# Expert slots in two tiles of 128, routed in three steps inside the attention, and partial value products in place of copies

## The chip, the cores and the metric

One core of a Trainium2 chip. The metric is the device time of one execution in microseconds (us), taken as the median of the runs shown; shorter is better.

## The reference

Attention over 4 batches, 8 heads, 768 positions, head width 64. Three heads (0, 2, 6) attend to every earlier position; the other five, the streaming heads, only to the last 64 positions and to positions 0 to 3. Then every token (3072 rows of 512 values) may pass through one of 8 experts:

```python
scores = where(mask, (q @ k.T) / sqrt(64), -1e9)
x = (softmax(scores) @ v)              # 3072 x 512 after the heads are joined
do_compute = x @ w_skip > 0            # the other tokens leave as they are
logits = x[do_compute] @ w_gate        # 8 experts, the largest is taken
y = gate * (relu(x @ w1[e]) @ w2[e])   # w1: 512 x 1024, w2: 1024 x 512
out[do_compute] = x[do_compute] + y
```

All inputs are float32; the kernel works in float16 with float32 sums.

## The kernel before

**The order of work is planned.** Each piece of work is registered with `op(name, engine, duration, function, deps, key)` or `dma(...)`. `Plan.lay` then runs a small list scheduler over these durations: on each engine, of what is ready, the piece with the smallest `key` goes first. The program is written in the order of the planned start times, and each engine works through its own list in that order. A wait on the chip therefore holds everything behind it on that engine. `fill` keeps weight loads from running far ahead of other transfers, and `pl.quiet` names two stretches in which no weight load is started: from the last pair's logits to the last attention write, and from the slot numbers (`idx`) to the second gather.

**Attention** runs over 16 pairs of heads, four pairs a batch (`i`, lines 701 to 1005). For each pair:

- `q`, `k` (queue of SyncE, buffers for four pairs) and `v` are loaded and cast to float16 on POOL (`cast` L690, `cast_v` L696), turned by TensorE (L715, L726), and copied out of PSUM: `q` by ACT (L741), `k` in two halves by DVE (L749), each half into a tile whose other 64 rows are zero.
- The gate's logits are carried along: `v` times the gate's weights (L778) stands beside the values in `va` (L785), ten columns for each head, so that the product with the attention weights yields rows, sums and logits at once.
- For streaming heads, `copy_kx` (L760, L761) builds keys for the previous block's second half with the four sink positions in front, and `copy_vx` (L796, L798) builds the same for the values: rows 64 to 127 from the previous block, rows 0 to 63 from block 0. Both on POOL.
- Scores (masks L853, products L865) go to PSUM in pieces of 1024 columns, ACT takes the exponential (L875), `weigh` (L920) multiplies with the values; every product there has all 128 rows.
- DVE takes the reciprocal of the sums (L939), scales logits (L946) and rows (L956). After a batch's last pair `g_sum` (L983) adds up its logits and SyncE's queue writes its rows to `out` (L977). The last batch is written in four parts, after pairs 13, 14 and 15 (twice).

**Routing** comes in two steps: batches 0 to 2 (18 chunks of 128 tokens) as filler in the last pairs, batch 3 (6 chunks) after the attention. A step finds each token's expert (`mx` to `oh`), its rank among the tokens of that expert by products with a triangle and with ones (`ranks`, L1055 to L1062), and then two tables, `L` (the rank as one of 128 positions) and `R` (the expert's tile, with token number and gate). The product of the two (`slots`, L1152) is the list of tokens by slot; `fin` (L1204 to L1207) makes `idx` and `gsl` of it. Each expert has 256 slots, two tiles of 128; tile `t` belongs to expert `t // 2`.

**Experts.** `swap` closes the pools of the attention and lays the expert's buffers over them: ten tiles of weights stay outside, the others and all gathered rows lie in the old attention memory. `gather` (L1239) fetches 128 rows of `out` by `idx`, one indirect transfer a tile on POOL, into rows zeroed by ACT (L1234). For each expert: cast (L1266), four transposes (L1275), copy (L1286); the first layer with both tiles at once, 256 columns, `hps` (L1295); ReLU on ACT (L1306); the second layer tile by tile, `yps` (L1317), always after the next expert's first layer; scaling and adding on DVE (L1323); `scatter` back to `out` (L1252).

**Weights** 0 to 13 (two for each expert, 2 MB of float32 each) are loaded and cast by POOL's queue (L479); 0 to 8 have room during attention, 9 lies in the old `v` buffer, the rest wait for `swap`. Weights 14 and 15 come as float32 on SyncE's queue (L1354), are staged in the space of experts 0 and 1 once these are done, and are cast by ACT and DVE (L1364, L1362).

Of the kernel before, what the change touches and what calls it, by code (L numbers as in the profile page):

```python
# [19 lines left out]
H = 8  # L20
# [25 lines left out]
CH = 1024  # L46

# [5 lines left out]
class Plan:  # L53
# [26 lines left out]
    def lay(self, rings):  # L80
# [30 lines left out]
        while n < len(self.ops):  # L111
            best = None
            for eng, c in ready.items():
                ts = [x for x in map(at, c) if x is not None]
                if ts:
# [7 lines left out]
                    key=lambda o: (o["key"], o["seq"]))  # L123
# [265 lines left out]
def kernel(  # L389
# [54 lines left out]
    cnt = const.tile([P, 2, E + 1], FP16, name="cnt")  # L444
# [15 lines left out]

    for e in range(2):
        t = wpool.tile([P, 2, DS * F], FP16, tag=f"w_{e}", name=f"w_{e}")
        for half in range(2):
            wts[e, half] = t[:, half]
    for n in range(4, NPRE):
        wtile(n, wpool)
# [21 lines left out]
    with tc.tile_pool(name="sm", bufs=1) as sm_pool, \  # L488
         tc.tile_pool(name="tr_ps", bufs=2, space=bass.MemoryType.PSUM) as tr_psum, \
         ExitStack() as pools, ExitStack() as pools2:  # L490

        def pool(name, stack=pools, **kw):
            return stack.enter_context(tc.tile_pool(name=name, **kw))

        ldq_pool = pool("ldq", bufs=1)
# [3 lines left out]
        st_psum = pool("st_ps", bufs=2, space=bass.MemoryType.PSUM)  # L499
# [3 lines left out]
              for n in range(2)]  # L503
# [4 lines left out]
        vxb = [qk_pool.tile([P, 2, NQB - 2, VA], FP16, name=f"vx{n}")  # L508
               for n in range(2)]
# [91 lines left out]
        def c_route():  # L601
# [10 lines left out]
            nc.gpsimd.memset(c24[:, :, 1:2], float(NC) / P)  # L612

        op("route0", "POOL", 2.2, c_route, [("Cv", 3)], 31)

        def c_route1():
            nc.vector.tensor_copy(iota16, tmpi)
            nc.vector.tensor_scalar(C.erev, tmpi[:, :E], -1.0, float(E),
                                    ALU.mult, ALU.add)
            nc.vector.tensor_copy(val[:, :, 1], tmpc)  # L620
            nc.vector.tensor_copy(val[:, :, 0], tmpp.to_broadcast([P, NC]))
# [17 lines left out]
        def load_qk(i, w, eng):  # L639
            def go():  # L640
                b, hs = heads(i)
                t = ldq_pool.tile([P, 2, NQB, D], FP32, tag=w + "f", bufs=NLD,
                                  name=w + "f")
# [13 lines left out]
        NLD = 4  # L657
        sp = iter(range(1000))
        for i in range(NPR):
            for w in "qk":  # L660
                act = i == 0 and w == "k"
                dma(("ld", w, i), "ACT" if act else "SP", 0.45, 1.07,
# [38 lines left out]
        for i in range(NPR):  # L701
            for w in "qk":
# [4 lines left out]
               [("ldv", 0, 1) if 0 < i < 4 else ("ldv", i // 4), ("PV", i - 3, 1), ("Vx", i - 3), "vones"],  # L707
# [37 lines left out]
        def out_k(i, hi):  # L745
            def go():
                r = slice(hi * D, (hi + 1) * D)
                to, ti = in_order(kz[i % 2][hi][r], tps["k", i][r])
                nc.vector.tensor_copy(to, ti)  # L749
# [40 lines left out]
        def copy_vx(i):  # L790
            def go():
                va, vx = vab[i % 3], vxb[i % 2]
                for hi in range(2):
                    if not retr(i, hi):
                        c = slice(hi * VA, (hi + 1) * VA)
                        nc.gpsimd.tensor_copy(  # L796
                            vx[D:, hi], va[D:, 1:NQB - 1, c])
                        nc.gpsimd.tensor_copy(  # L798
                            vx[:D, hi], va[:D, 0:1, c].to_broadcast(
                                [D, NQB - 2, VA]))  # L800
            return go

# [6 lines left out]
        for i in range(NPR):  # L809
# [7 lines left out]
            for hi in range(2):  # L817
                op(("Ok", i, hi), "DVE", 0.96, out_k(i, hi),
# [4 lines left out]
            op(("Tv", i), "PE", 0.36, transpose_v(i), [("Cv", i), "ident"],  # L823
# [6 lines left out]
            op(("Vx", i), "POOL", 0.95 * nx, copy_vx(i),  # L830
               [("Ow", i), ("PV", i - 2, 1)], k0 + 5)
# [67 lines left out]
        def weigh(i, hi):  # L899
            def go():  # L900
# [4 lines left out]
                va, vx = vab[i % 3], vxb[i % 2]  # L905
                vc = slice(hi * VA, (hi + 1) * VA)
                todo = []
                for qb in range(NQB):
                    if retr(i, hi):
                        todo += [(qb, RCOL[j, qb], va[:, j, vc])  # L910
                                 for j in range(qb + 1)]
                    else:
                        todo.append((qb, qb * P, va[:, qb, vc]))
                        if qb == 1:
                            todo.append((qb, NQB * P, va[:, 0, vc]))
                        elif qb:
                            todo.append((qb, (NQB - 1 + qb) * P,
                                         vx[:, hi, qb - 2]))
# [560 lines left out]
```

## Time and profile before

| | |
|---|---|
| median of 3 runs | 201.43 us (200.89 to 211.31) |
| the profiled execution | 200.39 us |
| its span, first to last instruction | 198.9 us |
| granted TensorE clock, mean over the span | 0.902 |
| TensorE busy | 151.8 us (76%) |
| POOL busy | 125.8 us (63%) |
| DVE busy | 115.3 us (58%) |
| ACT busy | 105.3 us (53%) |
| read from and written to DRAM | 56.64 MB, 10.49 MB |

"Busy" is the time in which an engine has at least one instruction in work; PE is TensorE, PEld its loading of weights. A name such as L1295 is a line of the kernel. In a group, the last column is the idle time of the engine just before, and what ended it. In a listing in order of time, each line has its start, its length, engine, line, operation, what is written and read, and in brackets the idle time before. Shares are over the whole span and hide that its stages have different limits, so they are read stage by stage.

### The profile page before, as it was taken

What the parts mean: (1) busy time and instruction counts of PE and PEld (TensorE: products, weight loads), DVE (VectorE), ACT (ScalarE), POOL (GpSimd) and SP (SyncE); (2) the same over time, 40 slices, a digit from 0 to 9 for tenths busy, and PEclk for the clock granted to TensorE, in tenths of its full rate; (3) what the DMA queues carried; (4) which work ended last, traced back from release to release, by engine and by line L of the source; (5) the groups of instructions that cost most, each with busy time, mean ns of one, the idle gap of its engine ahead of it and who ended that gap; (6) DMA issues with size and microseconds to landing.
All of it is one profiled execution on the core that took longest, in us unless ns stands there. A gap on an engine that the chain in (4) does not pass through costs nothing.

```text
span 198.9 us, 4630 instructions
## 1 busy us (share of the span) xinstructions
PE 151.8 (76%) x1832; PEld 119.5 (60%) x1832; DVE 115.3 (58%) x244; ACT 105.3 (53%) x137; POOL 125.8 (63%) x212
## 2 busy tenths in 40 slices
PE   0696789998999999999220027999999759699940
PEld 0475678787888888788220015978669247374810
DVE  6728687699788887998893033392664601304330
ACT  2178359986799789898389001534134013076500
POOL 7445997999889999986954187877835230101740
PEclk9999999999999999999955555899999957999995
DMA  4999999899989999999999439999999999960210
GB/s 158 320 340 347 339 376 331 279 308 338 340 224 356 268 331 212 213 278 282 237 276 250 82 85 243 272 192 285 269 340 405 244 247 269 242 162 9 72 64 15
DMA packets 28240, 49.21 MB, mean 247 GB/s; under 512 B 5156, under 2 KB 21412, under 8 KB 26930
## 3 DMA queue, kind: packets, MB, share of 16 engines
q0 software_dynamic: 5728, 19.45, 43.8%
q1 hardware_dynamic: 21152, 28.97, 43.3%
q10 hardware_dynamic: 1330, 0.41, 0.9%
q8 instruction: 16, 0.26, 0.6%
q14 instruction: 14, 0.11, 0.2%
HBM read 56.64 MB, written 10.49 MB: 337 GB/s over the span
## 4 chain that ended last, share of the span: by engine, by line
PE 45%; issue 20%; POOL 10%; DMA 8%; DVE 7%; SPq 3%; ACT 3%; POOLq 1%; ACTq 0%; DVEq 0%
PE hps L1295 10%; PE pst L865 9%; PE opsa L920 6%; PE yps L1317 6%; PE pst L853 6%; DMA kf<-in_k_dram 4%; PE tps L715 4%; POOL out_dram L1252 3%; DMA out_dram<-x 2%; DVE k L749 2%; SPq L644 2%; POOL q L690 2%; PE tps L726 2%; DMA xg<-out_dram,idx 2%; PE xtp L1275 2%
## 5 line engine op out<-in xcount | busy, mean ns | idle before, releaser
L875 ACT ACTIVATE at<-pst 128x1024 f16<-128x1024 f32 (+1 forms) x60 | 58.4, 1013 | 14.0 <-PE pst L865 13.1
L1306 ACT ACTIVATE ht<-hps 128x512 f16<-128x512 f32 x32 | 19.1, 597 | 55.4 <-PE hps L1295 46.4
L1295 PE MATMUL hps<-xT,w 128*128 128x256 f16 x256 | 34.8, 301 | 5.4 <-DMA w<-in_moe_w_dram 5.4
L865 PE MATMUL pst<-qT,k 128*128 128x128 f16 (+2 forms) x308 | 36.7, 240 | 2.1 <-ACT qT L741 0.9
L1295 PEld LDWEIGHTS <-w 128*128 128x128 f16 x256 | 31.0, 149 | 9.4 <-DMA w<-in_moe_w_dram 6.4
L1252 POOL DMA_INDIRECT out_dram<-xg,idx x16 | 16.5, 1034 | 29.2 <-issue 13.8
L749 DVE COPY k<-tps 64x768 f16<-64x768 f16 x32 | 30.4, 952 | 7.0 <-PE tps L715 6.6
L865 PEld LDWEIGHTS <-k 128*128 128x128 f16 x308 | 24.9, 101 | 11.0 <-DVE k L749 2.5
L1317 PE MATMUL yps<-w,ht 128*128 128x512 f16 x128 | 29.1, 379 | 0.2 <-ACTq L1441 0.2
L1239 POOL DMA_INDIRECT xg<-out_dram,idx x16 | 17.3, 1079 | 12.0 <-issue 11.7
L1323 DVE SCALAR_TENSOR_TENSOR xg<-yps,gsl,xg 128x512 f32<-128x512 f32 x16 | 12.0, 750 | 21.1 <-PE yps L1317 20.8
L853 PE MATMUL pst<-smask,identb 128*128 128x512 bf16 (+2 forms) x64 | 22.1, 356 | 0.2 <-ACT at L875 0.2
L920 PE MATMUL opsa<-va,at 128*128 128x74 f16 x392 | 19.5, 196 | 1.5 <-DVE x L956 1.5
L1317 PEld LDWEIGHTS <-ht 128*128 128x128 f16 x128 | 12.3, 98 | 13.6 <-issue 0.5
L920 PEld LDWEIGHTS <-at 128*128 128x128 f16 x472 | 18.0, 97 | 2.0 <-DVE x L956 1.8
L1286 DVE COPY xT<-xtp 128x512 f16<-128x512 f16 x16 | 6.3, 422 | 19.9 <-PE xtp L1275 19.5
L1266 DVE CAST x<-xg 128x512 f16<-128x512 f32 x16 | 9.9, 640 | 13.1 <-issue 10.0
L479 POOL DMA_DIRECT2D w<-in_moe_w_dram x22 | 12.8, 581 | 6.7 <-DMA w<-in_moe_w_dram 6.0
L741 ACT COPY qT<-tps 128x768 f16<-128x768 f16 x16 | 12.8, 800 | 7.2 <-PE tps L715 7.2
L1275 PE MATMUL xtp<-ident,x 128*128 128x128 f16 x64 | 6.0, 236 | 12.9 <-DVE x L1266 12.9
L696 POOL CAST va<-vf 128x768 f16<-128x768 f32 x16 | 13.3, 829 | 1.6 <-PE opsa L920 0.7
L956 DVE TENSOR_TENSOR x<-opsa,recs 128x768 f32<-128x768 f32 x15 | 14.2, 946 | 0.0
(128 smaller groups left out, 241.9 us busy)
## 6 DMA issues: line engine op xcount, KB each, us to landing
w<-in_moe_w_dram POOLq DMA_DIRECT2D x16, 512.0 KB
qf<-in_q_dram SPq DMA_DIRECT2D x16, 384.0 KB, 5.7
w<-in_moe_w_dram POOLq DMA_DIRECT2D x6, 1024.0 KB
kf<-in_k_dram SPq DMA_DIRECT2D x15, 384.0 KB, 6.1
out_dram<-x SPq DMA_DIRECT2D x7, 768.0 KB, 9.9
w<-in_moe_w_dram SPq DMA_DIRECT2D x4, 1024.0 KB, 13.3
kf<-in_k_dram ACTq DMA_DIRECT2D x1, 384.0 KB, 4.6
vf<-in_v_dram SPq DMA_DIRECT2D x1, 384.0 KB, 5.5
```

The lines of the kernel that those rows point to most:

```text
L696: nc.gpsimd.tensor_copy(vab[i % 3][:, :, GX:GX + 2 * D].rearrange("p n (h d) -> p h n d", h=2), fp32_of("v", i))
L749: nc.vector.tensor_copy(to, ti)
L853: nc.tensor.matmul(pst[:, c0 - c * CH:c0 - c * CH + m].rearrange("p (n c) -> p n c", c=P), identb, mv, start=(n == 0), stop=(n == last))
L865: nc.tensor.matmul(pst[:, c0 - c * CH:c0 - c * CH + m * P], lt, qTs[i][:, qb * P:(qb + m) * P], start=(n == 0), stop=(n == last))
L875: nc.scalar.activation(ats[i][:, c * CH:c * CH + cn], psts[i, c][:, :cn], ACT.Exp, scale=SCALE)
L920: nc.tensor.matmul(opss[i][:, hi, qb * VA:(qb + 1) * VA], ats[i][:, b0 + c:b0 + c + P], vb, start=(n == 0), stop=(n == len(todo) - 1))
L956: nc.vector.tensor_mul(xsb[i // 4][:, :, h0 * D:(h0 + 2) * D].rearrange("p n (h d) -> p h n d", h=2), summed(i, GX, 512 - GX, D), recs[:, ...
L1239: h = nc.gpsimd.indirect_dma_start(out=M.xgs[:, t], out_offset=None, in_=out[:, :], in_offset=bass.IndirectOffsetOnAxis(ap=idx[:, t:t + 1] ...
L1252: h = nc.gpsimd.indirect_dma_start(out=out[:, :], out_offset=bass.IndirectOffsetOnAxis(ap=idx[:, t:t + 1], axis=0), in_=M.xgs[:, t], in_of ...
L1295: nc.tensor.matmul(hps[:, fi, :], w1[:, s, 2 * f2 + fi], xTs[e][:, s, :], start=(fi == 0 and s == 0), stop=(fi == 1 and s == DS - 1))
L1306: nc.scalar.activation(hts[e][:, 2 * f2:2 * f2 + 2], hpss[e, f2], ACT.Relu)
L1317: nc.tensor.matmul(ypss[t], hts[e][:, j, s2 * P:(s2 + 1) * P], w2[:, j], start=(j == 0), stop=(j == FS - 1))
```

## The change

- **Values.** `copy_vx` and its buffers go. In a streaming head each product with such a copy becomes two into the same sum: rows 64 to 127 of the previous block, and rows 0 to 3 of block 0.
- **Slots.** An expert's two tiles are now `t = e` and `t = 8 + e`. The first 128 tokens of an expert fill tile `e`, counted over batches 0 to 2 alone; what is left of these and batch 3 go to tile `8 + e`.
- **Routing** has three steps: batches 0 and 1 (12 chunks, after pair 7), batch 2 (6 chunks, after pair 11), batch 3 (6 chunks). After step 1 the list of tiles 0 to 7 is complete. Step 2 needs only tiles 8 to 15; it starts each expert's count at `base1`, and has fewer operations. Each step has PSUM results of its own, added up in SBUF.
- **Experts** run in the order of `GR`: tile 0 to 3 of experts 0 to 3, each alone with 128 columns in the first layer; then tiles 8 to 11 of the same experts; then experts 4 to 7 with both tiles. Tiles 0 to 7 are gathered once batch 2 is written and step 1 is done; they go into the memory in which `q` and `k` arrived. The first layer uses the PSUM of the scores and may start after the last exponential; the second layer waits for `swap`. The hidden values of the first four lie in a buffer of the attention weights.
- **Copies of `k`.** For pairs 12 to 15 the second half's copy moves from DVE to ACT.
- **Writes.** The last batch goes out in three parts instead of four: 384 columns after pair 14, and twice 128 after pair 15.
- **Weights.** `quiet` is empty. Weights 14 and 15 are staged in four pieces where weights 8 to 11 lay, so each waits for expert 4 or 5 to be done with both tiles. `fill` lets weights from 7 on run 4 us ahead instead of 3, and this from weight 7 instead of 9.

The diff, cut:

```diff
+STEPS = ((0, 12), (12, 6), (18, 6))
+NSPLIT = 4
...
+        OK_ACT = (12, 13, 14, 15)
...
-                nc.vector.tensor_copy(to, ti)
+                (nc.scalar.copy if act else nc.vector.tensor_copy)(to, ti)
...
-        def copy_vx(i):
...
-                        nc.gpsimd.tensor_copy(
-                            vx[D:, hi], va[D:, 1:NQB - 1, c])
-                        nc.gpsimd.tensor_copy(
-                            vx[:D, hi], va[:D, 0:1, c].to_broadcast(
-                                [D, NQB - 2, VA]))
...
-                            todo.append((qb, (NQB - 1 + qb) * P,
-                                         vx[:, hi, qb - 2]))
+                        c = (NQB - 1 + qb) * P
+                        todo += [(qb, c, slice(D, P), qb - 1), (qb, c, slice(N_SINK), 0)]
+                for n, (qb, c, r, j) in enumerate(todo):
                     nc.tensor.matmul(
                         opss[i][:, hi, qb * VA:(qb + 1) * VA],
-                        ats[i][:, b0 + c:b0 + c + P], vb,
+                        ats[i][r, b0 + c:b0 + c + P], va[r, j, vc],
...
-        for i, u, c0, c1, took in ((13, None, 0, 256, 2.2), (14, None, 256, 384, 1.3),
+        for i, u, c0, c1, took in ((14, None, 0, 384, 3.1),
                                    (15, 0, 384, 512, 0.65), (15, 1, 384, 512, 0.65)):
...
+                "base": lambda: v.tensor_scalar(
+                    base1[:, :E], T[1, "rk"][:, n * E:(n + 1) * E], -float(P), 0.0,
+                    ALU.add, ALU.max),
...
-        for ph, c0, n, k0, last in ((0, 0, 18, 140, ("Gs", 2)),
-                                    (1, 18, 6, 150, ("Gs", 3))):
+        for (ph, (c0, n)), (k0, k1), last in zip(
+                enumerate(STEPS), ((105, 110), (130, 125), (150, 165)),
+                (("Gs", 1), ("Gs", 2), ("Gs", 3))):
...
+            for nm in (["rsel", "rank", "h128", "r16", "tt", "oht", "b8", "a8", "ob", "oa"],
+                       ["rsel", "base", "rank", "h128", "r16", "tt", "oht"],
+                       ["rsel", "place"])[ph]:
...
+        GR = [(e, (e,)) for e in range(NSPLIT)] + [(e, (E + e,)) for e in range(NSPLIT)]
+        GR += [(e, (e, E + e)) for e in range(NSPLIT, E)]
+        TO = [t for _, ts in GR for t in ts]
...
+                    hpss[g, u // 2] = st_psum.tile([P, CH], FP32, tag="pst", name="hps")
...
+                        T["hA"] = at_pool.tile([P, RLEN + SLEN], FP16, tag="at", name="hA")
...
+            dma(("G", t), "POOL", 1.1, 0.45, gather(t),
+                ["z" if ROW[t] >= NROW else None,
+                 *([("idx", 2), *X3] if t >= E else [("idx", 1), ("xo", 2, 0), ("xo", 2, 1)]),
...
+                (125 + x if t < NSPLIT else 400 + x), first=True)
...
+        STAGE = {(14, 0): 8, (14, 1): 9, (15, 0): 10, (15, 1): 11}
...
+                    [(prev, "go"), *(("Y", t, 1) for t in (e, E + e)),
...
+            k0 = 600 + 10 * g if t >= NSPLIT else 130 + x
+            op(("cx", t), "DVE", 0.62, cast_x(t), [("G", t), ("tx", back), "tables"], k0)
+            op(("tx", t), "PE", 0.25, turn_x(t), [("cx", t), ("ox", back)],
+               k0 - 15, take=("tps", ("ox", t)))
...
+                op(("F", g, u), "PE", 1.28 if len(ts) == 1 else 0.88, first(g, u),
+                   [("ox", ts[-1]), ("W", 2 * e, 0), ("W", 2 * e, 1),
                     *(("W", 2 * e, c // 2, c) for c in range(4)),
+                    ("X", NPR - 1, nch(NPR - 1) - 1)], k0,
+                   take=("pst", ("Re", g, u + 1)) if u % 2 == 0 else None)
...
-        pl.quiet = [(("Nl", NPR - 1), (("xo", 3, 15, 1), "go")),
-                    ("idx", (("G", 1), "go"))]
+        pl.quiet = []
```

## The prediction

> **What bounds the kernel now.** I read the 40 slices first, then busy time by stage, then the groups by shape, then the stretch between attention and the experts in order of time. The slices:
>
> ```profile
> PE   0696789998999999999220027999999759699940
> PEclk9999999999999999999955555899999957999995
> DMA  4999999899989999999999439999999999960210
> ```
>
> A slice is 4.97 us. TensorE is full to slice 19, nearly empty for four slices, then full again with one dent. The transfer engines are full nearly always; their one hole is slices 22 and 23. The granted clock is halved through the empty slices and one beyond.
>
> ```profile
> 60.00:80.00 20.00, 19.86 (x345) 17.02 (x342) 16.69 (x31) 17.53 (x21) 18.77 (x39) 1.00 1.06 288
> 80.00:97.40 17.40, 15.60 (x279) 13.38 (x280) 16.09 (x41) 12.67 (x15) 13.96 (x29) 1.00 1.06 255
> 97.40:121.00 23.60, 3.24 (x43) 2.56 (x43) 10.52 (x30) 10.34 (x21) 12.76 (x13) 0.53 0.77 179
> 121.00:157.00 36.00, 36.00 (x272) 27.71 (x271) 19.13 (x43) 11.89 (x20) 22.44 (x25) 0.93 1.02 288
> 157.00:177.40 20.40, 15.03 (x94) 10.90 (x93) 3.01 (x5) 4.44 (x8) 3.55 (x4) 0.83 1.00 242
> 177.40:191.40 14.00, 13.72 (x79) 7.91 (x77) 4.97 (x8) 8.37 (x11) 5.28 (x5) 1.00 0.13 44
> ```
>
> The columns are stretch, length, busy time of PE, weight load, DVE, ACT and POOL, clock, DMA share, GB/s. Attention (to 97.4) is bound by PE, 19.86 of 20 us. From 97.4 to 121.0 PE works 3.24 of 23.60 us. The experts are bound by PE to 157, by the arrival of weights to 177.4, and by PE again to 191.4. So there are two limits of almost one length, PE and the transfers, and both have their hole in the same place. What ends last in it:
>
> ```profile
> 97.43 0.23 DVE L939 RECIPROCAL recs<-opsa 128x12 f32<-128x12 f32 x1 [0.18 <-PE opsa L920]
> 98.96 1.35 DVE L1074 TENSOR_TENSOR r_sub<-glog,r_mx 128x48 f32<-128x48 f32 x1
> 107.03 0.19 DVE L1205 SCALAR_TENSOR_TENSOR idx<-msb 128x16 int32<-128x16 f32 x1
> 113.84 1.10 POOL L1239 DMA_INDIRECT xg<-out_dram,idx  x1 [7.09 <-issue]
> 117.33 1.15 DVE L1266 CAST x<-xg 128x512 f16<-128x512 f32 x2 [10.01 <-issue]
> 121.17 5.11 PE L1295 MATMUL hps<-xT,w 128*128 128x256 f16 x24
> ```
>
> Slots are known at 107.2, but the first gather waits until 113.84 for the last attention rows to land in DRAM (the chain of waits has that transfer from 101.86), and the first expert product comes 7.3 us after the gather.
>
> **Partial products.** The second value copies (20 x 0.43 + 20 x 0.43 us, 17.2 us of POOL) go. I credit nothing: POOL, 18.77 of 20 us busy, stands behind a PE that is fuller. If POOL were the true bound, up to 2 us more would be won in the last two batches. In exchange each of 80 products on 128 rows becomes two, on rows 64 to 127 and 0 to 3. A run of 32 such products takes 1.07 us in the chain of waits, 33 ns each, so 80 x 33 ns = +2.7 us of PE, hidden by nothing.
>
> ```profile
> L920 PE MATMUL opsa<-vx,at 128*128 128x74 f16 x80 | 7.9, 195 | 0.0
> L796 POOL COPY vx<-va 64x296 f16<-64x296 f16 x20 | 8.6, 432 | 1.9 <-DVE va L785 1.0
> L1295 PEld LDWEIGHTS <-w 128*128 128x128 f16 x256 | 31.0, 149 | 9.4 <-DMA w<-in_moe_w_dram 6.4
> L865 PEld LDWEIGHTS <-k 128*128 128x128 f16 x308 | 24.9, 101 | 11.0 <-DVE k L749 2.5 <-issue 2.3
> ```
>
> Every shape in the trace reads 128*128; it shows no product on fewer rows. From below: the two halves run side by side, +0 (a gain is excluded, since no product is saved). From above: each change of row count (full, 64, 4, full: 3 x 80 = 240) lets a product run out its 195 ns where 33 would do, 240 x 162 ns = +38.9 us. I take 2.7, by the nearest rows, and keep both ends.
>
> [...]
>
> **Routing in three steps.** Before the last PV, PE now issues ranks and slots of step 0 (12 + 13 products) and of step 1 (9 + 6), 40 against 18 rank products of the old first step. Eighteen slot products took 1.15 us (102.72), 64 ns each: 40 x 64 - 1.15 = +1.4 us. DVE: the old first step's rows add up to 5.5 us; steps 0 and 1 (12 and 6 chunks, the same rows scaled, plus a 0.95 us placement and the slot arithmetic) come to about 9, +3.5; against it four of the `k` copies (0.95 us) leave DVE, -3.8. They land on ACT as 4 x 0.80 = 3.2 us in the last four pairs, where ACT was busy 12.67 of 17.40; if those copies come on the path they cost up to those 3.2. So attention ends at 97.4 + 2.7 + 1.4 = 101.5.
>
> **The first four expert halves.** They need batch 2's rows in DRAM and step 1's slots. Batch 2's last normalization ended at 82.2; shifted by 3 and with the write's usual 9.9 us to landing that gives 95. Step 1 starts at about 84; the old first step took 11.6 us to its ranks among attention's DVE work, the new one is keyed ahead of the last pairs, so 10 us: slots at 94 to 95. Gathers on POOL (1.08 us each) from about 97. Old gathers reached their cast 3.5 to 4.1 us after issue; cast 0.62, four transposes 0.6, copy 0.42: first expert product at 103, after 1.5 us of idle PE.
>
> Its length: 32 products with 128 columns. Contiguous 128-column products go 4 in 0.22 us (55 ns); products with these strided weights go 32 in 3.49 us (109 ns, but for 256 columns). Strided loads last 144 ns at the median, others 98, 46 ns more; on top of the 33 ns of a PV step that makes 79 ns, which I take: 2.5 us a tile (1.8 to 3.5 by the ends). With the second layer (3.45 / 2 = 1.73) and transposes (0.22): 4.47 a tile, 17.9 for four. Half clock after the idle: 24 products once took 5.11 us instead of 2.62, but here the strided load hides part: +1.5. Step 2's 17 small products: +1.1. The early halves end at 103 + 20.5 = 123.5.
>
> **The later halves.** Step 2 has six chunks, shorter than before (the two 1.35 to 1.40 us vector operations that lay beside POOL's placements, four small ones and half of POOL's product go: 4 us). Worth nothing: the wait for the last rows hides it, and if that is gone it is worth those 4. The last rows leave 4.1 us later with attention; merging two writes puts 768 KB behind the last pairs, up to 2.6 us at 300 GB/s, and weights are no longer held back meanwhile. Gather at 113.84 + 4.1 + 0 to 2.6, first product 7.3 later: 125.2 to 127.9; I take 126, and PE is idle 2.5 us more.
>
> From there four half tiles 17.9, four whole experts 4 x (3.49 + 3.45) + 8 x 0.22 = 29.5: PE ends at 173.4. In the old run 7.5 us pass from the last product (191.4) to the end of the span (198.9): 180.9.
>
> **The transfers.** After 106 the shares sum to 66.8 us, at the usual 1.05 some 63.6 us of work; without the hole the last weights land at 106 + 63.6 = 169.6, and a cast (1.04) and half of the last second layer (1.7) make 172.4. So the second limit ends with the first, and the hole is all that can be won. Three waits are new. Weight 10's space holds the early halves' hidden values: free at 123.5, when weights 6 to 9 (18 us, with gathers and the last rows) are just through. The last expert's weights are staged where experts 4 and 5 lie and go out only after those are done: 155 and 162.8; two loads then take 5 to 7 us with the queue empty, landing at 170, nothing lost. If they take 12 to 14, as before (median 13.3), it is +5. POOL queues gathers and scatters behind these weight issues, none due then.
>
> **Sum.** 180.9 + 1.5 (200.39 - 198.9, around the span) = 182.4 beside the profiled execution's 200.39. The median of the runs is 0.5% above that execution: 183.4, 9% less than 201.43.
>
> **Rivals.** (1) *Changing row counts costs PE.* For: attention has no PE slack, the kernel builds copies and zeroed halves so that every product has 128 rows. Against: 472 products of this kind go at 33 ns whatever they read. Price 240 x the loss per change; at 75 ns it eats the whole 18 us and from 92 ns the kernel is over 2% slower; at 162 ns: 183.4 + 38.9 = 222. (2) *The early gathers hold attention.* DVE's cast and PE's transposes of the early tiles stand in order ahead of the last pairs' normalization and step 2; the plan gives a gather 2.35 us, the trace 3.5 to 5.4. Each of four can hold DVE up to 1.9 us, so 4 to 8 us: 187 to 191. Against: late gathers mostly meet an attention that is already over. (3) *The loads end last*: the staged weights' +5, perhaps a wait at weight 10 too: 188 to 190. (4) *The early halves do not start early*, because slots or rows come after 113: the gap stays, attention has +4.1, half tiles cost 8 x 2.5 - 4 x 3.49 = +6: 201.4 + 10 = 211. Against: batch 2's rows leave 20 us before batch 3's.
>
> **How the numbers follow.** Forecast (177 to 187) 0.44; rival 2 0.12; rival 3 0.10; rival 1 0.27, of which 0.07 stays within 2% and 0.20 beyond; rival 4 0.07. Within 2% is about what a measurement of this kernel can tell from no change. Faster 0.44 + 0.12 + 0.10 = 0.66, same 0.07, slower 0.27. Time: the forecast's 183.4. Range: down to 176 (products at 55 ns a column block, and the transfers' floor), up to 210, where the upper half of rival 1 and rival 4 stay out. The forecast's own range is 177 to 187.
>
> **What would show it.** Right: PV products with fewer rows at about 33 ns apart, 19.9 of 20 us PE in attention ending near 101; `hps` products with 128 columns from about 103, 79 ns apart; no DMA hole at 110 to 120; last product near 173. Wrong: PV groups of mixed rows far above 0.5 us, idle DVE before the first early cast with normalizations behind it, PE waiting for `w` beyond 165, or a first early gather after 110.

## The result: 220.4 us, 9.4% slower, and the profile after

The changed kernel takes 220.40 us (median; 219.97 to 222.2), the kernel before 202.09 beside it; the ratio is 1.094, interval 1.084 to 1.105. The prediction said 183.4 us, 176 to 210, and faster: wrong in sign and outside its range. The profiled execution of the change took 219.97 us, its span is 218.4 us. Some executions below take longer, most of them at a lower granted clock (213.09 us at 0.886 beside 209.73 at 0.917, the kernel before shifted by 64 bytes); the medians hold them, and every ratio with an interval leaves them out.

The slices of the changed kernel, 5.46 us each:

```profile
PE   0778789999999999999999869949899996476950
PEclk9999999799999999999999769997999999766997
DMA  6999999999999477869999996899999999992001
```

The stretch of four empty PE slices between attention and experts is gone, as the change wants. In its place attention is longer: PE is full to slice 21, 120 us, where it was full to 97. The transfers now have their holes in the middle of attention (the 4, 7, 7, 8 and 6 of slices 13 to 17, the first being 0), and but for slices 24 and 25 they are full to slice 35. By stage, with the columns of the prediction's table (length, busy time of PE, weight load, DVE, ACT and POOL, clock, DMA share, GB/s; DVE is VectorE, ACT ScalarE, POOL GpSimd, SP SyncE):

```profile
60.00:80.00 20.00, 19.92 (x265) 15.91 (x264) 13.26 (x26) 13.87 (x16) 9.83 (x18) 1.00 0.85 243
80.00:125.10 45.10, 44.22 (x585) 34.47 (x584) 29.60 (x76) 28.18 (x32) 30.43 (x46) 0.96 0.90 183
183.60:198.30 14.70, 6.66 (x33) 5.08 (x33) 0.75 (x1) 3.94 (x6) 1.35 (x2) 0.77 0.95 296
```

PE is the bound of attention, 19.92 of 20 us, to 125.1 (97.4 before). ACT and POOL have become idle beside it (busy 13.87 and 9.83 of the 20 us, 17.53 and 18.77 before). Near the end there is a stretch in which PE works 6.66 of 14.70 us while the transfers are busy. The value products by shape, columns as in the page's groups:

```profile
L916 PE MATMUL opsa<-va,at 128*128 128x74 f16 x392 | 28.8, 201 | 0.6 <-DVE x L952 0.4 <-PE pst L862 0.2
L916 PE MATMUL opsa<-va,at 64*128 64x74 f16 x80 | 16.3, 203 | 0.0
L916 PE MATMUL opsa<-va,at 4*128 4x74 f16 x80 | 16.2, 203 | 0.0
```

The products on 64 and on 4 rows last as long as those on 128 (203 against 201 ns), and hold PE 16 us each for 80 of them. The time of one streaming head is read from the timeline of PE, as the start of its 15 products and of the instruction behind them:

```profile
115.62 1.80 PE L916 MATMUL opsa<-va,at 128*128 128x74 f16 x15
117.35 0.39 PE L862 MATMUL pst<-qT,k 128*128 128x256 f16 x2
```

1.73 us. In the kernel before, the 11 products of a head took 0.37 us (59.88 to 60.25):

```profile
59.88 0.30 PE L920 MATMUL opsa<-va,at 128*128 128x74 f16 x4
...
60.22 0.20 PE L920 MATMUL opsa<-vx,at 128*128 128x74 f16 x1
60.25 0.38 PE L853 MATMUL pst<-rmask,identb 128*128 128x512 bf16 x1
```

Twenty heads times 1.36 us are 27.2 us, and attention ends 27.7 us later. (All value products together hold PE 46.5 us, 20.1 before: 26.4 more.) The last two waits of PE for weights, in its timeline:

```profile
188.80 6.61 PE L1349 MATMUL hps<-xT,w 128*128 128x256 f16 x32 [5.16 <-DMA w<-in_moe_w_dram]
198.32 5.25 PE L1384 MATMUL yps<-w,ht 128*128 128x512 f16 x16 [2.91 <-DMA w<-in_moe_w_dram]
```

Both are for the weights of expert 6, which come by GpSimd's queue. So two things are to be explained: 27 us of attention, and why the stretch from attention's end to PE's last product, 94.0 us before and 71.9 predicted, is 86.0 us.

### The profile page after: what moved, and what is told of

Same layout as the page of the kernel before. It is cut to its first block, busy times and chain, and to the rows that moved or that the text cites. A ratio compares the mean times of both kernels' runs of the same rounds, so it can differ in the third digit from the quotient of the medians.

```text
span 218.4 us, 5017 instructions
## 1 busy us (share of the span) xinstructions
PE 183.7 (84%) x2043; PEld 139.3 (64%) x2043; DVE 114.4 (52%) x259; ACT 101.9 (47%) x135; POOL 107.2 (49%) x172
## 3 DMA queue, kind: packets, MB, share of 16 engines
q1 hardware_dynamic: 20368, 28.97, 43.7%
## 4 chain that ended last, share of the span: by engine, by line
PE 44%; issue 28%; DVE 12%; POOL 8%; DMA 3%; POOLq 1%; ACT 1%; DVEq 0%; ACTq 0%
PE opsa L916 18%; PE pst L862 10%; PE pst L850 6%; POOL out_dram L1297 5%; PE tps L722 4%; PE hps L1349 2%; PE tps L733 2%; DMA rows<-in_q_dram 2%; POOL w L483 2%; DVE k L759 2%; DMA rows<-out_dram,idx 2%; DVE x L952 1%; DVE x L1310 1%; PE vw L788 1%; DVE va L795 1%
## 5 line engine op out<-in xcount | busy, mean ns | idle before, releaser
L916 PE MATMUL opsa<-va,at 128*128 128x74 f16 x552 | 46.5, 201 | 0.6 <-DVE x L952 0.4
L916 PEld LDWEIGHTS <-at 128*128 128x128 f16 x552 | 34.5, 97 | 11.4 <-issue 1.1
L1369 ACT ACTIVATE ht<-hps 128x512 f16<-128x512 f32 x24 | 13.3, 596 | 44.9 <-PE hps L1349 35.2
L1297 POOL DMA_INDIRECT out_dram<-rows,idx x12 | 12.0, 1004 | 44.4 <-DVE rows L1390 38.4
L1349 PE MATMUL hps<-xT,w 128*128 128x128 f16 (+1 forms) x256 | 26.6, 265 | 6.8 <-DMA w<-in_moe_w_dram 5.2
L1390 DVE SCALAR_TENSOR_TENSOR rows<-yps,gsl,rows 128x512 f32<-128x512 f32 x12 | 9.0, 751 | 30.4 <-PE yps L1384 30.3
L697 POOL CAST q<-rows 128x768 f16<-128x768 f32 x15 | 12.4, 828 | 11.6 <-PE tps L722 7.9
L1288 POOL DMA_INDIRECT rows<-out_dram,idx x12 | 12.9, 1074 | 5.2 <-issue 3.4
L697 POOL CAST k<-rows 128x768 f16<-128x768 f32 x15 | 12.4, 829 | 5.7 <-PE tps L722 3.0
L779 DVE COPY vT<-tps 128x768 f16<-128x768 f16 x16 | 8.9, 554 | 11.6 <-PE tps L733 11.5
## 6 DMA issues: line engine op xcount, KB each, us to landing
w<-in_moe_w_dram SPq DMA_DIRECT2D x4, 1024.0 KB, 15.6
out_dram<-x SPq DMA_DIRECT2D x1, 1152.0 KB, 10.6
```

The source lines that it names most:

```text
L697: e.tensor_copy(t, fp32_of(w, i).rearrange("p h n d -> p n h d"))
L916: nc.tensor.matmul(opss[i][:, hi, qb * VA:(qb + 1) * VA], ats[i][r, b0 + c:b0 + c + P], va[r, j, vc], start=(n == 0), stop=(n == len(todo) ...
L1297: moved(nc.gpsimd.indirect_dma_start(out=rows_of(t), out_offset=bass.IndirectOffsetOnAxis(ap=idx[:, t:t + 1], axis=0), in_=row(t), in_offs ...
L1349: nc.tensor.matmul(hps[:, j], w1[:, s, u * nj + j], xTs[g][:, s, :m], start=(j == 0 and s == 0), stop=(j == nj - 1 and s == DS - 1))
L1369: nc.scalar.activation(hts[g][:, u * nj:(u + 1) * nj, :m], hpss[g, u // 2][:, c:c + 512].rearrange("p (j m) -> p j m", m=m), ACT.Relu)
```

## Experiments

Theory A: each change of row count costs TensorE some 0.1 us. Rivals: B, products on fewer rows are slow themselves; C, it is their number, or their summing into one place; D, the loss is in what the change does elsewhere. For the stretch behind attention, T (the transfers set its end) stands against the order of gathers, casts and products (C in that run's text).

### What the partial products cost

**Partial products alone, in the kernel before.** The value copies and their waits go, the 80 products are split, nothing else.

```diff
-   todo.append((qb, (NQB - 1 + qb) * P, vx[:, hi, qb - 2]))
+   c = (NQB - 1 + qb) * P
+   todo += [(qb, c, slice(D, P), qb - 1), (qb, c, slice(N_SINK), 0)]
```

> The kernel before with the partial products alone. Theory A: 20 streaming heads x 1.36 us = +27 us of PE in an attention that has no slack; attention ends near 124 instead of 97.4 and the time is 224 to 232 us. Theory D: +2.7 us for 80 more products, 203 to 206 us.

221.94 us, ratio 1.114 (1.105 to 1.122); attention's last value product starts at 122.9 (97.2 before). The time is 2 us under theory A's range, far from D's. This part alone makes the kernel as slow as the whole change does. D falls.

**The copies back, in the changed kernel.**

```diff
-   todo += [(qb, c, slice(D, P), qb - 1), (qb, c, slice(N_SINK), 0)]
+   todo.append((qb, c, None, qb - 2))          # one product from vx
+   op(("Vx", i), "POOL", 0.95 * nx, copy_vx(i), ...)
```

> The changed kernel with the second value copies back on POOL, so that every product in attention has 128 rows again; all else of the change stays (one logits buffer instead of two, to make room). Theory A, the changes of row count cost PE about 0.1 us each, 240 of them: the 11 value products of a streaming head take 0.37 us again instead of 1.73, attention ends near 100 us instead of 125.1, and the time falls to 185 to 195 us, below the kernel before. Theory D, the rest of the change is what costs (routing inside the attention, early gathers, late loads): attention still ends after 110 and the time stays above 202.

212.12 us, ratio 1.065 (1.056 to 1.075). The value products are back at 0.37 us a head, yet 8 us were won, not 25 to 35. The timelines of POOL and of PE show why:

```profile
107.38 1.08 POOL L1306 DMA_INDIRECT rows<-out_dram,idx  x1 [6.23 <-DMA out_dram<-x]
...
117.63 0.39 POOL L772 COPY kx<-k 64x256 f16<-64x256 f16 x1 [4.38 <-DMA rows<-out_dram,idx]
```

```profile
118.22 0.60 PE L879 MATMUL pst<-qT,kx 128*128 128x128 f16 x4 [14.56 <-POOL kx L773]
```

The first early gather waits on GpSimd for batch 2's rows to land, until 107.38. Behind it in that queue stand the other gathers and pair 15's key copy, and PE stands 14.56 us for that copy. That is the prediction's rival 2 (early gathers hold attention), in another queue than the one it named and at twice its price. The changed kernel does not show it, because its attention is late enough for the gathers.

**A head's products sorted by row count**: the same 15 products, seven on 128 rows, four on 64, four on 4, so three changes a head in place of twelve.

```diff
+   todo.sort(key=lambda o: -(o[2].stop - (o[2].start or 0)))
```

> The changed kernel with the products of a streaming head in another order: the seven of 128 rows first, then the four of 64 rows, then the four of 4 rows, so 3 changes of row count a head instead of 12. Theory A (each change costs about 0.1 us): 9 x 20 x 0.1 = 18 us less PE, a head in about 0.8 us instead of 1.73, attention ends near 107 and the time is 196 to 205 us. Theory B (each product on fewer rows is itself slow, about 0.19 us, in any order): a head still takes 1.73 us and the time stays near 220.

206.58 us, ratio 1.034 (1.022 to 1.047). A head takes:

```profile
102.30 0.87 PE L917 MATMUL opsa<-va,at 128*128 128x74 f16 x15
103.11 0.39 PE L862 MATMUL pst<-qT,k 128*128 128x256 f16 x2
```

From start to next start that is 0.81 us (0.80 to 0.81 in the other heads) in place of 1.73, and attention ends at 107.8; the time is 2 us above theory A's range. The products on few rows are the same, so B falls. Fifteen products at 33 ns are 0.50 us; the rest is 1.23 us over 12 changes in the one order, 0.31 us over 3 in the other: 0.10 us a change in both. The products on few rows also begin at other rows than the full ones do (64 to 127, 0 to 3), and no run parts the number of rows from their place.

**Both partial products over all 128 rows.**

```diff
-   todo += [(qb, c, slice(D, P), qb - 1), (qb, c, slice(N_SINK), 0)]
+   todo += [(qb, c, slice(P), qb - 1), (qb, c, slice(P), 0)]
```

> The changed kernel with both partial products of each group read over all 128 rows: as many products as in the change, none on fewer rows (the sums then hold value rows that do not belong to them). Theory A and theory B: 15 products of a head in 0.5 us, attention ends near 102, time 186 to 197 us. Theory C, that it is the number of products or their summing into one place that costs: a head still takes over 1.5 us, time near 220.

On these sums the kernel runs a second, general path too, and its 4237 us contain it; only its attention is read. A head takes 0.50 us there, in the order of the change and into the same sums:

```profile
68.35 0.67 PE L916 MATMUL opsa<-va,at 128*128 128x74 f16 x15
68.85 0.50 PE L722 MATMUL tps<-ident,k 128*128 128x128 f16 x6
```

All value products hold PE 23.2 us (20.1 before, 46.5 in the change) and end at 105.7, where some 102 was expected. C falls: 80 more products cost 3.1 us, 39 ns each, near the 2.7 us that the prediction took. The changes of row count, with the place of the rows, are the rest.

### A hidden cost: where the V slabs lie

In the changed kernel the loads of the first 30 us were slow: with the transfer engines full (share 1.09 to 1.14), 215 to 224 GB/s for several us at a time, 331 to 348 before. The SP queue's packets took 95.4 us of the 16 engines (43.7% of 218.4), before 86.1 (43.3% of 198.9), for the same bytes. One theory was the single tile `rows`; the other that the new constants `base1` and `tcode` move every later tile up by 64 bytes, the V slabs from byte 97536 to 97600 of a partition. One row of V is 256 bytes, and 97536 is 381 times 256.

**The kernel before, shifted by 64 bytes.**

```diff
+   const.tile([P, 32], FP16, name="pad64")
    cnt = const.tile([P, 2, E + 1], FP16, name="cnt")
```

> The kernel before with one unused tile of 64 bytes ahead of the counts, so that every later tile lies 64 bytes higher, as the change's new constants have it: the V slabs at byte 97600 (a multiple of 64) where they were at 97536 (a multiple of 128). Nothing else is changed. Theory P (the place of the V slabs makes their loads slow): 217 to 223 GB/s for several us at a time while a V load runs, against 331 to 348 in the kernel before; the SP queue's share of 16 engines goes from 43.3% of 198.9 us (86.1 us) to 94 to 97 us; the time rises by 0 to 8 us (201 to 210), little if the weights behind have slack. Theory R (the one tile for all query and key rows is the cause): nothing changes, 86 us of queue time, 199 to 203 us.

210.52 us, ratio 1.044 (1.036 to 1.053). GB/s from 2 to 42 us, 1 us a figure, first the shifted kernel, then the kernel before:

```profile
GB/s 138 318 375 270 193 270 310 311 217 218 219 216 224 355 376 370 366 272 216 219 217 230 213 227 295 369 370 373 372 373 363 378 348 245 224 218 215 218 222 177
```

```profile
GB/s 92 316 384 286 303 334 337 341 338 340 242 398 389 318 365 365 340 338 340 313 327 361 363 389 378 363 374 374 366 322 331 337 260 103 267 398 324 353 247 293
```

The plateaus (figures of 213 to 230) come with 64 unused bytes alone; the kernel before has none, its 5th to 32nd figures are 303 to 398 but for one of 242. The queue's share, 45.3% of 211.6, is 95.9 us. The tile `rows` has no part in it.

**The grouped order, shifted by another 64 bytes** (V at 97664, a multiple of 128), by the same unused tile.

> The grouped order (three changes of row count a head) with the same 64 bytes added, which puts the V slabs at byte 97664, a multiple of 128 again; the query and key rows still lie in one tile. Theory P: no stretches at 218 GB/s in the first 30 us, queue time of SP back from 95.7 us to 85 to 88 us, attention's last product at 105 to 107 us instead of 107.8, and the time, whose last stages wait for weights, 197 to 203 us against 206.6 of the grouped order without the shift. Theory R: 218 GB/s and 95 us of queue time stay, and the time stays at 205 to 208.

207.09 us, ratio 1.022 (0.998 to 1.045), plateaus unchanged (213 to 230 GB/s), theory P's figures missed. A multiple of 128 is not enough.

**The two constants moved to the later pool**, V at 97536 again, in the changed kernel and in the grouped order.

```diff
-   base1 = const.tile([P, E + 1], FP16, name="base1")
-   tcode = const.tile([P, NT], FP16, name="tcode")
+   base1 = sm_pool.tile([P, E + 1], FP16, name="base1")
+   tcode = sm_pool.tile([P, NT], FP16, name="tcode")
```

> The changed kernel with its two new constants (base1, tcode) taken from the later pool, so that the V slabs lie at bytes 97536 and 109824 again, as in the kernel before (multiples of 256; the shift by 64 bytes to a multiple of 128 alone did not help). The shift by 64 bytes cost the kernel before 4.4% (some 9 us). Theory P2 (the slabs must lie at a multiple of 256, the length of one of their rows): no stretches at 218 GB/s in the first 30 us, 85 to 88 us of SP queue time in place of 95.4. Of the time then 4 to 10 us come back: 210 to 216 us, since in the changed kernel too the transfers end late; what is left over the kernel before is the price of the partial products. If TensorE alone sets the changed kernel's time: 218 to 222 us at the faster loads. If the place of the slabs isn't it: 218 GB/s stays and 218 to 222.

> The same move of the two constants in the grouped order (three changes of row count a head). Theory P2: 85 to 88 us of SP queue time, attention's last product at 105 to 108 us, 195 to 202 us against 206.6 of the grouped order at the shifted place. Otherwise 204 to 208.

The plateaus are gone (from 6 to 12 us 306 to 346 GB/s in both, 303 to 341 in the kernel before, 197 to 325 in the change), and SP's share is 86.3 us (39.3% of 219.5) and 84.2 us (41.0% of 205.3). The times stay: 220.85 (ratio 1.099, 1.093 to 1.105) and 207.30 (1.025, 0.993 to 1.058). The 4 to 10 us that theory P2 hoped for do not come: where PE is the bound of attention, faster loads won nothing. So this cost is real, and not what made the change slow.

### What sets the end without the partial products

**Copies back, early gathers behind pair 15's key copy**, without and with the 64 bytes.

```diff
+   *([("Kx", 15)] if t < NSPLIT else []),                  # gather's waits
-   [("G", t), ("tx", back), "tables"], k0)                  # early cast
+   [("G", t), ("tx", back), "tables", *([("Nl", 15)] if t < NSPLIT else [])], k0)
```

> The changed kernel with the second value copies restored, and with the four early gathers kept behind pair 15's key copy on GpSimd and the four early casts behind pair 15's logits on VectorE (in the copies-back experiment the first gather's wait for batch 2's writes held that key copy, and TensorE stood 14.6 us for it). Theory A2 (the order on GpSimd alone was what the copies-back experiment lost): TensorE's wait of 14.6 us is gone, attention's last product at 101 to 104 us instead of 121.6, and the time 191 to 200 us. Theory W (the weights set the end by themselves, since the first of them is issued late and their loads are slow): attention ends at 101 to 104 all the same, TensorE then waits for weights, and the time is 203 to 212.

> The kernel of the run before with the 64 bytes added, so that the V slabs lie at a multiple of 128. If both theories hold (order on GpSimd, place of the V slabs): attention's last product at 100 to 102 us, 9 to 10 us less of queue time on SP, and 184 to 194 us, faster than the kernel before. If the weights are late for another reason: 197 to 205 us.

209.99 us (1.047, 1.033 to 1.061) and 211.01 (1.043, 1.023 to 1.063): missed, and they tell little. The gather of expert 4, which I had not bound, still stood ahead of pair 15's value copy, and PE now waited for that one, 14.5 and 16.7 us. (In both the swap of pools also waits for the first early product.)

**All gathers of first tiles behind both copies, V at byte 97536 again.**

```diff
-   *([("Kx", 15)] if t < NSPLIT else []),
+   *([("Kx", 15), ("Vx", 15)] if t < E else []),
-   [("F", 0, 0), *((n, "go") for n in X3)], lat=0.0)        # swap's waits
+   [("Re", 0, 0), *((n, "go") for n in X3)], lat=0.0)
```

> The copies restored, the two constants moved, and all the gathers of first tiles behind both copies of pair 15 on GpSimd (in the last such runs one gather, of expert 4, still stood ahead of pair 15's value copy, and TensorE stood 14.5 and 16.7 us for that copy). Theory A2 and P2 together: no wait of TensorE above 3 us before attention's last product, which comes at 99 to 102 us; SP queue time 85 to 88 us; 186 to 195 us, faster than the kernel before. If the stretch after attention needs 94 us as in the kernel before whatever comes earlier: 195 to 198. If the weights' loads end late for another reason: 200 to 210.

200.52 us, ratio 0.992 (0.986 to 0.998): attention ends at 102.6, the wait is gone, and this repaired version is level with the kernel before. But PE's last product ends at 190.3, 87.7 us after attention, not the 72 of the prediction. Its timelines, POOL and then PE:

```profile
104.03 1.09 POOL L1306 DMA_INDIRECT rows<-out_dram,idx  x1 [3.96 <-DMA out_dram<-x]
```

```profile
110.88 0.61 PE L1337 MATMUL xtp<-ident,tables 128*128 128x128 f16 x4 [5.03 <-DVE tables L1328]
112.00 3.57 PE L1367 MATMUL hps<-tables,w 128*128 128x128 f16 x32 [0.52 <-issue]
...
172.12 5.06 PE L1367 MATMUL hps<-xT,w 128*128 128x256 f16 x32 [6.40 <-DMA w<-in_moe_w_dram]
```

The first expert product comes at 112.0, 9 us before the old kernel's 121.2, and the gain is lost again at 172, to a weight of expert 6. The forecast that fits is the last one, that loads end late for another reason.

**The same with V shifted by 64 bytes**, to part the two edits.

```diff
-   base1 = sm_pool.tile([P, E + 1], FP16, name="base1")     # and tcode
+   base1 = const.tile([P, E + 1], FP16, name="base1")
```

> The same version (200.5 us) with only the two small constants back in the first pool, so that the V slabs lie 64 bytes higher, at byte 97600. If the place of the slabs is worth what it was worth in the kernel before (4.4%): stretches at 218 GB/s in the first 40 us, SP queue time of 95 us in place of 86.6, and 205 to 210 us. If the order on GpSimd alone made the step from 210 to 200.5: 199 to 202 us.

SP's queue takes 96.0 us again. The median is 206.33; the fastest execution, of 200.2 us, lies within the 198.1 to 201.6 of the unshifted version. By it the step from 210 to 200.5 came from the order on GpSimd, together with the swap's other wait. One execution is a thin base, and as the other three take 204.9 to 208.0 us, it stays open whether the place of the slabs had a part in the step.

**The last expert's weights left out.**

```diff
-   w1 = wts[e, 0].rearrange(...)
+   w1 = wts[min(e, E - 2), 0].rearrange(...)                # w2 likewise
-   for n in (14, 15):                                       # loads and casts
+   for n in ():
```

> The version with copies, gathers behind and slabs home (200.5 us), but the last expert's weights are not loaded and not cast; its products use the weights of the expert before it. It leaves out 4.2 of 49.2 MB of transfers and eight casts of 0.95 us (six on ScalarE, two on VectorE); TensorE does the same number of products. The four loads were among the last to land, 15.6 us each at the median beside other transfers. Theory T (after attention the transfers set the end; in all the kernels they add up to 177 to 181 us of all 16 engines): TensorE's waits for weights beyond 165 us go, and the time is 187 to 193 us. Theory C (gathers, casts and products in their order set the end): 198 to 201 us.

189.95 us against 200.52: 10.6 us for 4.2 MB, PE's work unchanged, and no wait of PE for a weight beyond 155 us. Theory T holds and C falls: with the order of gathers and products kept, the end moves with the loads. Two limits: the two versions were not run beside each other, and the kernel before took 198.1 us beside this one (a single execution) and some 201.2 beside the other, so some 3 of the 10.6 us may be the occasion. And the queues' work falls by 6.5 us only (176.9 to 170.4); the run also takes out the late start of these four loads and their casts, which it does not part from their bytes.

**Weights let out earlier**, in the version of 200.5 and, alone, in the kernel before.

```diff
-   dma(("ld", w, i), ..., 0.45, 1.17, ...)                  # repaired version only
+   dma(("ld", w, i), ..., 0.45, 1.07, ...)
-   -60 + x, first=True, fill=1.5 if name[1] < 7 else 4.0)
+   -60 + x, first=True, fill=4.0)      # kernel before: 1.5 to 4.0 for weights 0 to 8
```

> The version with copies, gathers behind and slabs home (200.5 us), with the first weights let out earlier: the planner's time for a query or key load is 1.07 us again (1.17 in the change), and weights 0 to 6 go out when 4.0 us of transfers are still queued (1.5 before). Theory T: the transfer engines' shares of 0.86 to 0.99 between 20 and 80 us fill up, the first weight goes out before 60 us instead of at 67.5, and the end comes 2 to 4 us earlier: 196 to 199 us. If weights ahead of the key and value loads hold attention: 201 to 206 us.

> The kernel before with its first weights let out earlier (when 4.0 us of transfers are still queued, 1.5 before), nothing else. Theory N (in the kernel before the transfers stand still between attention and the experts because nothing may be loaded then, so weights that come earlier only make that hole longer): 199 to 203 us. Theory O (earlier weights help by themselves): 194 to 198 us.

194.47 us (192.56 to 194.89), the best version of the change and below what theory T forecast; the kernel before beside it took 198.07 us in one execution and 201.96 to 209.28 in the other six, so there is no interval. The kernel before with earlier weights takes 195.32 us (193.47 to 195.78), ratio 0.982 (0.970 to 0.993). Theory N, which I thought the likelier, falls: earlier weights help by themselves. With them the repaired change and the old kernel are level, as far as versions that were not run beside each other show it. The stages show what the early halves change in the transfers; the version of 200.5 first, then the one of 194.5:

```profile
0.00:106.00 106.00, 84.66 (x1364) 70.42 (x1379) 83.88 (x189) 76.09 (x96) 84.90 (x170) 1.00 0.96 279
106.00:125.00 19.00, 12.98 (x137) 10.66 (x138) 8.54 (x22) 5.36 (x8) 15.76 (x17) 0.73 0.86 247
```

```profile
0.00:106.00 106.00, 87.00 (x1349) 72.52 (x1365) 81.70 (x180) 73.29 (x83) 85.24 (x172) 0.97 1.01 289
106.00:125.00 19.00, 8.97 (x112) 8.15 (x109) 8.79 (x28) 4.55 (x17) 14.92 (x16) 0.64 0.96 261
```

The kernel before has 1.01 up to 106 us and 0.69 from 106 to 125. The first version fills 3.2 us of the old hole (0.17 of 19 us) and has 5.3 us less done before it (0.05 of 106 us). In both versions GpSimd's queue issues no weight between 102 and 116 us; it works off gathers there. The second version has both, the fuller hole and as much done before it as the kernel before. Over the whole span the queues' shares sum to 176.6 us of all engines in the kernel before, 176.9 and 176.4 in these two, 175.8 in the old kernel with earlier weights.

**Three last runs.** Weights 0 to 6 earlier still; the changed kernel with partial products and earlier weights; the version of 194.5 with V shifted.

```diff
-   -60 + x, first=True, fill=4.0)
+   -60 + x, first=True, fill=8.0 if name[1] < 7 else 4.0)   # the first; also casts behind the swap
```

> The version of 194.5 us (copies, gathers behind, slabs home, weights earlier) with weights 0 to 6 let out when 8.0 us of transfers are queued, 4.0 there. The transfer engines were idle some 6 us between 120 and 180 us there, and full before: 193 to 196 us if nothing more is to be won, 190 to 193 if the first weights were still late, 196 to 202 if the key and value loads are now held.

> The changed kernel, partial products kept, with its weights let out earlier in the same way. In the changed kernel the transfer engines' share was 0.85 and 0.76 between 60 and 100 us, and its last weights came late. If TensorE alone sets its time: 217 to 221 us as without. If late weights set its last stretch: attention's last product still at 125 to 126 us, and 208 to 214 us.

> The version of 194.5 us with only the two small constants back in the first pool, the V slabs 64 bytes higher. The loads of the V slabs then take 9 to 10 us more of all 16 engines. If the transfers bound this version from end to end: 199 to 205 us. If there is enough idle time in the transfers to take it: 193 to 197 us.

225.85 us (ratio 1.128) and 236.27 us (1.186), far above every forecast. In both PE stands 18.3 and 19.6 us for the first early cast, which waits for its gathered rows, and after that the transfers' share falls to 0.27 (140 to 160 us in the one, 74 GB/s; 160 to 180 in the other, 48 GB/s). Both runs also hold the later casts until the pools are swapped, and in the second the swap waits for the first early ReLU, so they mix several edits; they show that this order is bad, and leave open whether the change as it stands lost its last stretch to late weights. With V shifted the version of 194.5 has a ratio to the kernel before of 0.993 (0.985 to 1.001), from three executions of 196.3 to 198.9 us: there the place of the slabs costs some 3 us (middle of the three 197.4, against 194.5 on another occasion).

## Why the prediction was wrong

- **Attention bound by PE**: right, 19.92 of 20 us from 60 to 80.
- **Partial products, +2.7 us**: the step that failed. They cost 27.2 us. The text had both ends (0 and 38.9), as suppositions that no row of the trace showed, with the changes of row count as the cause of the upper one, and took 2.7 "by the nearest rows". Those rows, 33 ns a product, all have 128 rows and never change row count, so they priced the number of products and said nothing of the changes. The all-rows run shows the part that they do price, 3.1 us. Of the 37 us, 24.5 are this term: with it attention's end would have been put at 126.0, and it is 125.1.
- **Copies removed, credited nothing**: right in the change; with the copies back attention ends at 102.6, and POOL does not limit it once the gathers are out of the way.
- **Routing, +1.4 us of PE**: not too small as PE's work, but that was not all. In the version of 200.5 PE works 84.3 us until attention ends, 83.8 in the kernel before; yet attention ends at 102.6 and not at the 98.8 of the sum without partial products, because PE waits 4.9 us more. Of its waits, those for DVE's key copies before the scores grew to 3.8 us (0.6 before), and one for the first routing step (1.1) is new.
- **Early halves from 103**: in the change 128.0, since attention lasts to 125.1; in the repaired version 112.0. What failed there is the landing of batch 2's rows: put at 95 with a write of 9.9 us, it held the first gather to 104.03; the writes took 16.3 us at the median.
- **79 ns for a 128-column product**: somewhat too high, 66 ns measured in the change (32 in 2.12 us).
- **Transfers, "the hole is all that can be won", last weights at 169.6**: the second failed step, most of the other 13 us. The stretch behind attention is 14.1 us longer than the sum had it, and PE's waits for weights in it, of which the sum had none, are 9.5 us. The sum moved the hole's time to the front of the queue and took it that the rest stays. In the repaired versions the transfers' work stayed at 176 to 177 us, but the hole gave back 3.2 us and time was lost elsewhere in the same queue. In the change the work even grew, to 191.1 us (181.5 with V at its old place, where the time was the same). What made the weights of the change itself late was not isolated: the run that was to show it mixed several edits.
- **Staged weights, "nothing lost, else +5"**: these loads took 15.6 us at the median, the condition of the "else". But PE's waits (5.16 and 2.91 us in the change, 6.40 in the repaired version) are for expert 6's weights, which were on their way by GpSimd's queue at the same time; for the staged ones PE waits 0.4 and 1.6 us. With the staged loads left out the 6.40 go too.
- **Rivals**: rival 1 (row counts), at 222 us, is what came, though its number is partly luck: 24.5 us from the row counts at 0.10 us each, not 38.9, and most of the rest is late loads, rival 3's theme, at more than its price. Rival 2 is real, and hidden in the change by rival 1. The sign of rival 4 was there in the change (first early product at 128), but as a result of rival 1, not of late rows: the first early gather, at 116.9, waits there for no transfer. I gave the right one 0.27.

## What to carry over

A row of the profile prices an instruction only within the pattern it stands in: if the edit changes the pattern (here the row count from one product to the next), its price is the unknown (33 ns in the row, 0.10 us more at each change); here the middle of the two bounds would have been nearer than the end with the familiar number. When two resources are full for almost the whole span, the idle stretch of one is not yet time won (3.2 us came of the hole here): sum the busy time of both, and ask where in the queue time is lost, before promising the hole. Small tiles put in front of a pool move everything behind them (64 bytes made some 340 GB/s some 218 here), so compare the addresses of what is loaded in short rows before and after.

## What the runs showed of the hardware

- A change of row count between two products (no run parts the number of rows from their place) cost 0.10 us of TensorE (12 a head: 1.73 us; 3 a head: 0.81; none, on all rows: 0.50), while the products on fewer rows lasted as long as those on 128, 203 against 201 ns.
- Loads whose rows are 256 bytes ran at some 218 GB/s with the tile that they write at byte 97600 or 97664, and at some 340 (331 to 348 in the kernel before) at 97536. No run shows why. Three places are a small sample, and the shift moved other tiles with the slabs.
- That loss of some 10 us of transfer time cost nothing where PE was the bound (220.85 against 220.40), some 1.5% (197.4 against 194.5, on two occasions) in the best version, and 4.4% in the kernel before; in the version of 200.5 one execution (200.2) shows no loss.
